# A two-layer SiLU block on one core: matmuls that reuse the weights already loaded

## The chip, the core and the metric

The kernel runs on one core of a Trainium2 chip. TensorE multiplies a stationary operand ("weights", loaded by an instruction of its own) with a moving operand and writes into PSUM, which has 8 banks of 512 fp32 columns here. ScalarE (ACT) and VectorE (DVE) read PSUM and write SBUF. The SP and ACT queues issue DMAs. The metric is the device time of one execution in microseconds; the time before is the median of three runs.

## The reference

The inputs are bf16: x is 1 x 2048 x 640 (S = 2048 tokens, D = 640), w1 is 640 x 1728, w2 is 1728 x 640 (F = 1728).

```python
def reference(x, w1, w2):
    h = jnp.einsum("bsd,df->bsf", x, w1)
    h = _silu(h)
    out = jnp.einsum("bsf,fd->bsd", h, w2)
    return out
```

## The kernel before

All operands stay in SBUF. `xT` holds x transposed, 5 blocks of 128 rows of D by 2048 tokens. `w1s` holds w1 in 5 such blocks. h is kept transposed: `hT` has 13 tiles of 128 rows of F by 2048 tokens, and the last 64 rows of F go to `hTt`, two chunks side by side in the two halves of the partitions. w2 is `w2s` (13 tiles of 128 rows) and `w2t` (the last 64 rows, loaded twice, once in each half).

**First product.** The tokens are taken in four chunks of 512 (`SCH`). Chunk 0 is interwoven with the loads of w1. Then one loop runs over chunks 1, 2 and 3: for each of 13 tiles of F it takes a bank, issues 5 matmuls (one for each block of D; the w1 tile is the stationary operand, 512 columns of `xT` the moving one), and a Silu on ACT writes the tile of `hT`. `wait(pe, ld_xc[c])` ahead of each chunk waits for that chunk's five x transposes, which SP issues early on, chunk after chunk (line 158). The last 64 rows of F follow for all chunks (`h_tail`), two chunks at a time in the two halves of the array's columns.

**Second product, last 128 columns (`Wide`).** For each chunk, `Wide(c)` computes the last 128 of 640 output columns, transposed: the stationary operand is a half tile of w2 (64 rows by 128 columns), the moving one 512 tokens of `hT`. Two units run at once, one on rows 0 to 63 of the array (r0 = 0) and one on rows 64 to 127 (r0 = `HP`), each into its own bank. Each unit must see both halves of every tile, so it makes two passes: `begin` with one half and then its 64-row `tail`, whose last matmul ticks `halfway`; `rest` with the other half. The second pass of a unit must not start before its first has been written, which is what `wait(pe, X.halfway, Y.halfway)` in `quad` is for. `quad` runs the first pass of units 0 and 1, the first pass of 2 and 3, then the second pass of 0 and 1, and the second pass of 2 and 3, closing each unit behind its second pass. `close` copies the bank to `oT` (`evac` alternates between DVE and ACT), and SP transposes it by DMA into `o_sb` (line 275).

**Second product, first 512 columns (`Tok`).** For each block of 128 tokens the stationary operand is a tile of `hT` and the moving one 512 columns of w2. Three quads of half-row units follow, and the last four blocks use whole rows, the very last split in 384 and 128 columns. Each block is copied and stored; a store waits for its chunk's output transpose (`st_w`).

The order of the work is written out by hand: each engine takes its instructions in program order, and every dependence is a semaphore wait by `wait`. `bank()` hands out the 8 banks in turn and makes PE wait until the last reader of the bank is done. All matmuls are recorded under line 170, in `mm`. Each `pe.matmul` becomes two instructions, a weight load and a matmul.

Of the kernel before, what the change touches and what calls it, by code (L numbers as in the profile page):

```python
# [9 lines left out]
def bass_standalone__dense_activation_silu__prompt_kernel(  # L10
# [11 lines left out]
    S, D = xf.shape  # L22
    F = w1.shape[1]
    P = 128
    NB = 8
    BANK = 512
    DT = D // P
    FT = F // P
    FL = F - FT * P
    SCH = 512  # L30
    HB = 256
    NSC = S // SCH
    DA = 512
# [4 lines left out]
    pe, act, dve, pool, sp = nc.tensor, nc.scalar, nc.vector, nc.gpsimd, nc.sync  # L38

    with ExitStack() as es:  # L40
        def sb(name, shape, dtype):
            return es.enter_context(nc.sbuf_tensor(name, shape, dtype))

        xT = sb("xT", [P, DT, S], bf16)
        w1s = sb("w1s", [P, DT, F], bf16)
        w2s = sb("w2s", [P, FT, D], bf16)
        w2t = sb("w2t", [P, D], bf16)
        hT = sb("hT", [P, FT, S], bf16)
        hTt = sb("hTt", [P, NSC // 2, SCH], bf16)
# [4 lines left out]
        ps = es.enter_context(nc.psum_tensor("ps", [P, NB, BANK], fp32))  # L54
# [4 lines left out]
        def sem(name):  # L59
            s = es.enter_context(nc.semaphore(name))  # L60
            count[s.name if hasattr(s, "name") else name] = 0
            return [s, 0]

        def tick(ins, s, n=1):
            ins.then_inc(s[0], n)
            s[1] += n
            return (s, s[1])

        def wait(eng, *points):
            for pt in points:  # L70
                if pt is None:
                    continue
                s, v = pt
                key = (id(eng), id(s))
                if seen.get(key, 0) < v:
                    eng.wait_ge(s[0], v)
                    seen[key] = v

        s_pe, s_act, s_dve = sem("s_pe"), sem("s_act"), sem("s_dve")
# [74 lines left out]
        ld_xc = {}  # L154
# [14 lines left out]
        def mm(o, l, r, start, stop, shared=False):  # L169
            return pe.matmul(o, lhsT=l, rhs=r, start=start, stop=stop, skip_group_check=shared)  # L170

        def silu(out_ap, in_ap, bank, after):
            wait(act, after)
            r = tick(act.activation(out=out_ap, in_=in_ap, func=ACT.Silu), s_act)  # L174
            bank_free[bank] = r
            return r

        def part(k, ft, c0, c1, start=False, stop=False):
            return mm(ps[:, ft, c0:c1], w1s[:, k, ft * P:(ft + 1) * P], xT[:, k, c0:c1],
                      start, stop, shared=True)  # L180
# [14 lines left out]
        for ft in range(NO):  # L195
            t = tick(part(4, ft, 0, SCH, stop=True), s_pe)
            silu(hT[:, ft, 0:SCH], ps[:, ft, :], ft, t)
# [3 lines left out]
        def bank():  # L201
            b = nxt[0] % NB
            nxt[0] += 1
            wait(pe, bank_free[b])
            return b

        wait(pe, ld_rest)
        for ft in range(NO, FT):
            b = bank()
            if ft == NO + 2:  # L210
                wait(pe, ld_rest2)
            for k in range(DT):
                ins = mm(ps[:, b, :], w1s[:, k, ft * P:(ft + 1) * P], xT[:, k, 0:SCH],
                         start=(k == 0), stop=(k == DT - 1))
            silu(hT[:, ft, 0:SCH], ps[:, b, :], b, tick(ins, s_pe))
        for c in range(1, NSC):
            wait(pe, ld_xc[c])
            for ft in range(FT):
                b = bank()
                for k in range(DT):  # L220
                    ins = mm(ps[:, b, :], w1s[:, k, ft * P:(ft + 1) * P],
                             xT[:, k, c * SCH:(c + 1) * SCH], start=(k == 0), stop=(k == DT - 1))
                h_last = silu(hT[:, ft, c * SCH:(c + 1) * SCH], ps[:, b, :], b, tick(ins, s_pe))
        h_tail = []
        for q in range(NSC // 2):
            b = bank()
            for k in range(DT):
                for hh in range(2):
                    c = 2 * q + hh
                    ins = mm(ps[hh * FL:(hh + 1) * FL, b, :], w1s[:, k, F0:F],  # L230
                             xT[:, k, c * SCH:(c + 1) * SCH],
                             start=(k == 0), stop=(k == DT - 1), shared=True)
# [16 lines left out]
        HP = P // 2  # L249
# [4 lines left out]
        class Wide:  # L254
# [3 lines left out]
            def open(self):  # L258
                self.b = bank()

            def half(self, r0, ft, start, stop):
                c = self.c
                return mm(ps[:, self.b, :], w2s[r0:r0 + HP, ft, DA:D],
                          hT[r0:r0 + HP, ft, c * SCH:(c + 1) * SCH], start, stop, shared=True)

            def tail(self):
                q, r0 = self.c // 2, (self.c % 2) * FL
                return mm(ps[:, self.b, :], w2t[r0:r0 + FL, DA:D], hTt[r0:r0 + FL, q, :],
                          False, False, shared=True)

            def close(self, t):
                c = self.c
# [44 lines left out]
        def lanes(up, down):  # L317
            for i in range(max(len(up), len(down))):
                for lane in (up, down):
                    if i < len(lane):  # L320
                        lane[i]()

        def begin(u, r0):
            def end():
                wait(pe, *h_tail)
                u.halfway = tick(u.tail(), s_pe)
            return [lambda ft=ft: u.half(r0, ft, ft == 0, False) for ft in range(FT)] + [end]

        def rest(u, r0, done):
            ops = [lambda ft=ft: u.half(r0, ft, False, ft == FT - 1) for ft in range(FT - 1)]  # L330
            ops.append(lambda: done.append(tick(u.half(r0, FT - 1, False, True), s_pe)))
            return ops

        def quad(A, B, C, E):
            A.open()
            B.open()
            lanes(begin(A, 0), begin(B, HP))
            C.open()
            E.open()
            lanes(begin(C, 0), begin(E, HP))  # L340
            for X, Y in ((A, B), (C, E)):
                dx, dy = [], []
                wait(pe, X.halfway, Y.halfway)
                lanes(rest(Y, 0, dy), rest(X, HP, dx))
                X.close(dx[0])
                Y.close(dy[0])

        wait(pe, *ld_w2)
        wait(pe, h_last)
        quad(Wide(0), Wide(1), Wide(2), Wide(3))  # L350
        last = None
        for q in range(NSC // 2):
            for j in range(0, JB, 2):
# [12 lines left out]
        for u, eng in ((A, dve), (B, act), (C, act), (E, dve), (G2, act)):  # L366
            for ft in range(FT):
                ins = u.whole(ft, ft == FT - 1)
# [31 lines left out]
```

## Time and profile before

| | |
|---|---|
| median of three runs | 124.97 us (124.93 to 125.05) |
| profiled execution | 124.80 us |
| its span, first to last instruction | 123.2 us |
| TensorE busy | 120.9 us, 797 matmuls and 797 weight loads |
| chunks 2 and 3 of the first product | 32.1 to 60.1 us |
| last-column units | 62.7 to 74.4 us |

The profile is one execution of the program. PE is the matmul row, PEld the weight loads, SPq and ACTq the DMA queues. Each group of instructions has its line, engine, operation, output and inputs, its count, busy time and mean duration, and the idle time of the engine just before with what ended it. The recorded end of a matmul is modelled, and consecutive matmuls overlap in the record (each lasts some 0.38 us, and they start closer together than that), so their distance from start to start is what counts. A slot here means the time from one matmul start to the next, where matmuls that run at the same time in two halves of the array are one slot.

### The profile page before, as it was taken

Reading aid. Unit: us, or ns where it says so; the run is one execution under the profiler, and the core shown is the slowest. Engines: PE = TensorE matmul, PEld = TensorE weight load, DVE = VectorE, ACT = ScalarE, POOL = GpSimd, SP = SyncE. Lnnn points to the kernel's source line nnn. Section 1 sums busy time; section 2 is a strip of 40 time slices with the busy share of each in tenths; the row PEclk is TensorE's granted clock in tenths of the full one; section 3 lists DMA queues with packets and bytes.
Section 4 is the critical chain, followed back from the end, with each engine's and each line's share of the span. In section 5 each row is a group of like instructions: output and inputs, shape, how many; then the busy total and the mean of one; then the engine's idle time right before and its main releaser. Section 6 shows DMA issues by size and latency. Waiting matters only on the chain.

```text
span 123.2 us, 1779 instructions
## 1 busy us (share of the span) xinstructions
PE 120.9 (98%) x797; PEld 55.5 (45%) x797; DVE 6.8 (6%) x11; ACT 38.8 (31%) x67; POOL 0.3 (0%) x5
## 2 busy tenths in 40 slices
PE   8999999999999999999999999999999999999993
PEld 6344444444444444444444444444444444444452
DVE  0000000000000000000000022002201300222001
ACT  4002975555555555555530011001101200110110
POOL 1000000000000000000000000000000000000000
PEclk9999999999999999999999999999999999999999
DMA  6999845445990000000000004202200220022122
GB/s 141 238 255 306 162 112 94 97 93 101 345 366 10 0 5 0 3 0 0 0 0 5 0 13 113 50 0 106 106 0 5 106 106 0 5 106 106 53 74 86
DMA packets 19479, 10.38 MB, mean 84 GB/s; under 512 B 13456, under 2 KB 18960, under 8 KB 19472
## 3 DMA queue, kind: packets, MB, share of 16 engines
q1 hardware_dynamic: 19184, 10.05, 31.1%
q10 hardware_dynamic: 288, 0.23, 0.7%
q8 instruction: 6, 0.10, 0.3%
q14 instruction: 1, 0.01, 0.0%
HBM read 4.51 MB, written 2.62 MB: 58 GB/s over the span
## 4 chain that ended last, share of the span: by engine, by line
PE 94%; DMA 3%; ACT 0%; issue 0%
PE ps L170 94%; DMA w1s<-in_w_dram 3%; ACT o_sb L244 0%
## 5 line engine op out<-in xcount | busy, mean ns | idle before, releaser
L170 PE MATMUL ps<-xT,w1s 128*128 128x512 bf16 (+1 forms) x280 | 59.1, 381 | 0.1
L170 PE MATMUL ps<-w2s,hT 64*128 64x512 bf16 (+3 forms) x377 | 46.2, 369 | 0.0
L170 PEld LDWEIGHTS ps<-xT,w1s 128*128 128x128 bf16 (+1 forms) x280 | 26.4, 99 | 32.7 <-DMA w1s<-in_w_dram 0.8
L174 ACT ACTIVATE hT<-ps 128x512 bf16<-128x512 f32 x52 | 30.0, 608 | 28.9 <-PE ps L170 28.9
L170 PEld LDWEIGHTS ps<-w2s,hT 64*128 64x128 bf16 (+1 forms) x377 | 21.0, 95 | 24.2 <-issue 0.2
L244 ACT CAST o_sb<-ps 128x512 bf16<-128x512 f32 (+1 forms) x9 | 4.9, 550 | 41.5 <-PE ps L170 41.5
L170 PE MATMUL ps<-hT,w2s 64*128 64x512 bf16 x104 | 11.7, 376 | 0.0
L170 PEld LDWEIGHTS ps<-hT,w2s 64*128 64x128 bf16 x104 | 5.0, 94 | 6.3 <-issue 0.4
L242 DVE CAST o_sb<-ps 128x512 bf16<-128x512 f32 (+1 forms) x8 | 5.4, 675 | 40.5 <-PE ps L170 40.5
L242 DVE CAST oT<-ps 128x512 bf16<-128x512 f32 x2 | 1.4, 692 | 73.7 <-PE ps L170 73.7
L244 ACT CAST oT<-ps 128x512 bf16<-128x512 f32 x2 | 1.2, 585 | 10.6 <-PE ps L170 10.6
L130 PE MATMUL ps<-z 128*128 128x256 bf16 x15 | 3.4, 419 | 0.4 <-DVE z L124 0.4
L170 PE MATMUL ps<-w2t,hTt 64*128 64x512 bf16 (+2 forms) x17 | 2.9, 363 | 0.0
L130 PEld LDWEIGHTS ps<-z 128*128 128x128 bf16 x15 | 2.1, 147 | 1.2 <-DVE z L124 0.4
L174 ACT ACTIVATE hTt<-ps 128x512 bf16<-128x512 f32 x2 | 1.2, 597 | 1.1 <-PE ps L170 1.1
L152 ACT ACT_TABLE_LOAD x1 | 1.3, 1283 | 0.7 <-PEq L385 0.7
L170 PEld LDWEIGHTS ps<-w2t,hTt 64*128 64x128 bf16 x17 | 0.9, 94 | 1.1
L170 PE MATMUL ps<-hTt,w2t 64*128 64x512 bf16 x4 | 0.8, 376 | 0.0
L170 PEld LDWEIGHTS ps<-hTt,w2t 64*128 64x128 bf16 x4 | 0.2, 94 | 0.2
L152 ACT ACTIVATE warm<-warm 128x32 f32<-128x32 f32 x1 | 0.2, 229 | 0.0
L139 POOL MEMSET warm<- 128x32 f32 x1 | 0.1, 124 | 0.3 <-POOLq L385 0.3
L385 POOL MEMSET const-bfloat16-1.0<- 128x1 bf16 x1 | 0.1, 101 | 0.0
(4 smaller groups left out, 0.4 us busy)
## 6 DMA issues: line engine op xcount, KB each, us to landing
out_dram<-o_sb SPq DMA_DIRECT2D x15, 160.0 KB, 1.8
w2s<-in_w_dram SPq DMA_DIRECT2D x1, 1120.0 KB, 6.4
w1s<-in_w_dram SPq DMA_DIRECT2D x4, 256.0 KB, 3.9
w2s<-in_w_dram SPq DMA_DIRECT2D x1, 960.0 KB, 8.6
w1s<-in_w_dram SPq DMA_DIRECT2D x1, 560.0 KB, 6.4
w1s<-in_w_dram SPq DMA_DIRECT2D x1, 320.0 KB, 5.2
xT<-in_x_dram SPq DMA_TRANSPOSE x18, 3.7
w1s<-in_w_dram ACTq DMA_DIRECT2D x1, 160.0 KB, 2.5
```

What stands on the lines that cost most here:

```text
L130: pe.matmul(ps[:, 3, 0:HB], lhsT=z[:, 0:1].broadcast_to([P, P]), rhs=z[:, 0:1].broadcast_to([P, HB]), start=True, stop=True)
L139: p_warm = tick(pool.memset(warm[:, :], 0.0), s_pool)
L152: act.activation(out=warm[:, :], in_=warm[:, :], func=ACT.Silu)
L170: return pe.matmul(o, lhsT=l, rhs=r, start=start, stop=stop, skip_group_check=shared)
L174: r = tick(act.activation(out=out_ap, in_=in_ap, func=ACT.Silu), s_act)
L242: r = tick(dve.tensor_copy(out=out_ap, in_=in_ap), s_dve)
L244: r = tick(act.copy(out=out_ap, in_=in_ap), s_act)
L385: nc = _bacc.Bacc("TRN2", target_bir_lowering=False, num_devices=1)
```

## The change

A new helper `held` emits a matmul without a weight load, so that it uses the weights that the matmul before it (on the same rows) left in the array. It is used in two places. In the first product, chunk 1 keeps its loop, and chunks 2 and 3 are taken together: for each tile of F two banks, and for each block of D one matmul with its load for chunk 2 and one `held` for chunk 3. PE waits for the x of both chunks ahead of the first tile, and the two Silu of a tile follow its last matmul.

The last-column units no longer go through `quad`. `wides` runs all four at once: for each tile, units 0 and 1 with loads on the two row halves, then units 2 and 3 `held` on the same halves; then the four tails in the same manner; then one wait for `halfway` of all four; then the second pass with the halves exchanged, and the four `close` at the end. The other quads are as before.

```diff
+        def held(o, l, r, start, stop, shared=False):
+            rows = l.shape[0]
+            r0 = l.base_partition()
+            return pe.add_instruction(mybir.InstMatmult(
+                name=nc.get_next_instruction_name(),
+                ins=[pe.lower_ap(r), pe.lower_ap(l)],
+                outs=[pe.lower_ap(o)],
+                start_tensor_calc=start, stop_tensor_calc=stop,
+                tile_size=(rows, P), tile_position=(r0, 0), ldweights=False,
+                bass_skip_group_check=shared,
+            ))
...
-        for c in range(1, NSC):
-            wait(pe, ld_xc[c])
-            for ft in range(FT):
-                b = bank()
-                for k in range(DT):
-                    ins = mm(ps[:, b, :], w1s[:, k, ft * P:(ft + 1) * P],
+        wait(pe, ld_xc[1])
...
+        wait(pe, ld_xc[2], ld_xc[3])
+        for ft in range(FT):
+            pair = [(c, bank()) for c in (2, 3)]
+            done = []
+            for k in range(DT):
+                for op, (c, b) in zip((mm, held), pair):
+                    ins = op(ps[:, b, :], w1s[:, k, ft * P:(ft + 1) * P],
                              xT[:, k, c * SCH:(c + 1) * SCH], start=(k == 0), stop=(k == DT - 1))
-                h_last = silu(hT[:, ft, c * SCH:(c + 1) * SCH], ps[:, b, :], b, tick(ins, s_pe))
+                    if k == DT - 1:
+                        done.append(tick(ins, s_pe))
+            for (c, b), t in zip(pair, done):
+                h_last = silu(hT[:, ft, c * SCH:(c + 1) * SCH], ps[:, b, :], b, t)
...
+        def wides():
+            us = [Wide(c) for c in range(NSC)]
+            for u in us:
+                u.open()
+            for ft in range(FT):
+                for u, r0, hold in ((us[0], 0, 0), (us[1], HP, 0), (us[2], 0, 1), (us[3], HP, 1)):
+                    u.half(r0, ft, ft == 0, False, hold)
+            wait(pe, *h_tail)
+            for u, r0, hold in ((us[0], 0, 0), (us[1], HP, 0), (us[2], 0, 1), (us[3], HP, 1)):
+                u.halfway = tick(u.tail(hold), s_pe)
+            wait(pe, *[u.halfway for u in us])
+            done = []
+            for ft in range(FT):
+                for u, r0, hold in ((us[1], 0, 0), (us[0], HP, 0), (us[3], 0, 1), (us[2], HP, 1)):
+                    t = u.half(r0, ft, False, ft == FT - 1, hold)
+                    if ft == FT - 1:
+                        done.append((u, tick(t, s_pe)))
+            for u, t in done:
+                u.close(t)
+
         wait(pe, *ld_w2)
         wait(pe, h_last)
-        quad(Wide(0), Wide(1), Wide(2), Wide(3))
+        wides()
```

`Wide.half` and `Wide.tail` take an argument `hold` that picks `held` instead of `mm`.

More of the change, by code (lines that the diff above doesn't have):

```diff
@@ L215, in bass_standalone__dense_activation_silu__prompt_kernel @@
             silu(hT[:, ft, 0:SCH], ps[:, b, :], b, tick(ins, s_pe))
-        for c in range(1, NSC):
-            wait(pe, ld_xc[c])
-            for ft in range(FT):
-                b = bank()
-                for k in range(DT):
-                    ins = mm(ps[:, b, :], w1s[:, k, ft * P:(ft + 1) * P],
+        wait(pe, ld_xc[1])
+        for ft in range(FT):
+            b = bank()
+            for k in range(DT):
+                ins = mm(ps[:, b, :], w1s[:, k, ft * P:(ft + 1) * P],
+                         xT[:, k, SCH:2 * SCH], start=(k == 0), stop=(k == DT - 1))
+            silu(hT[:, ft, SCH:2 * SCH], ps[:, b, :], b, tick(ins, s_pe))
+        wait(pe, ld_xc[2], ld_xc[3])
+        for ft in range(FT):
+            pair = [(c, bank()) for c in (2, 3)]
+            done = []
+            for k in range(DT):
+                for op, (c, b) in zip((mm, held), pair):
+                    ins = op(ps[:, b, :], w1s[:, k, ft * P:(ft + 1) * P],
                              xT[:, k, c * SCH:(c + 1) * SCH], start=(k == 0), stop=(k == DT - 1))
-                h_last = silu(hT[:, ft, c * SCH:(c + 1) * SCH], ps[:, b, :], b, tick(ins, s_pe))
+                    if k == DT - 1:
+                        done.append(tick(ins, s_pe))
+            for (c, b), t in zip(pair, done):
+                h_last = silu(hT[:, ft, c * SCH:(c + 1) * SCH], ps[:, b, :], b, t)
         h_tail = []
@@ L259, in open, with half, tail @@
                 self.b = bank()
-            def half(self, r0, ft, start, stop):
+            def half(self, r0, ft, start, stop, hold=False):
                 c = self.c
-                return mm(ps[:, self.b, :], w2s[r0:r0 + HP, ft, DA:D],
-                          hT[r0:r0 + HP, ft, c * SCH:(c + 1) * SCH], start, stop, shared=True)
-            def tail(self):
+                return (held if hold else mm)(
+                    ps[:, self.b, :], w2s[r0:r0 + HP, ft, DA:D],
+                    hT[r0:r0 + HP, ft, c * SCH:(c + 1) * SCH], start, stop, shared=True)
+            def tail(self, hold=False):
                 q, r0 = self.c // 2, (self.c % 2) * FL
-                return mm(ps[:, self.b, :], w2t[r0:r0 + FL, DA:D], hTt[r0:r0 + FL, q, :],
-                          False, False, shared=True)
+                return (held if hold else mm)(
+                    ps[:, self.b, :], w2t[r0:r0 + FL, DA:D], hTt[r0:r0 + FL, q, :],
+                    False, False, shared=True)
             def close(self, t):
@@ L346, in quad @@
                 Y.close(dy[0])
+        def wides():
[10 more added lines that the diff above has]
+            done = []
+            for ft in range(FT):
+                for u, r0, hold in ((us[1], 0, 0), (us[0], HP, 0), (us[3], 0, 1), (us[2], HP, 1)):
[4 more added lines that the diff above has]
+                u.close(t)
         wait(pe, *ld_w2)
         wait(pe, h_last)
-        quad(Wide(0), Wide(1), Wide(2), Wide(3))
+        wides()
         last = None
```

## The prediction

> **What bounds the kernel now.** I read the page's busy table and slices first, then the chain that ended last, then the stages one by one.
>
> ```profile
> PE 120.9 (98%) x797; PEld 55.5 (45%) x797; DVE 6.8 (6%) x11; ACT 38.8 (31%) x67; POOL 0.3 (0%) x5
> PE   8999999999999999999999999999999999999993
> PEclk9999999999999999999999999999999999999999
> PE 94%; DMA 3%; ACT 0%; issue 0%
> L170 PE MATMUL ps<-xT,w1s 128*128 128x512 bf16 (+1 forms) x280 | 59.1, 381 | 0.1
> L170 PEld LDWEIGHTS ps<-xT,w1s 128*128 128x128 bf16 (+1 forms) x280 | 26.4, 99 | 32.7 <-DMA w1s<-in_w_dram 0.8
> ```
>
> TensorE is busy nearly everywhere, and its matmuls are 94% of the chain. The weight loads (PEld) last 99 ns each but have a row of their own beside the matmuls; whether they cost anything is seen only in the distance from one matmul to the next. So I asked for the stages: first chunks 1, 2 and 3 of the first product, then the last-column units.
>
> ```profile
> 18.05:32.08 14.03, 14.03 (x66) 6.37 (x65) 0.00 (x0) 7.76 (x13) 0.00 (x0) 1.00 0.56 118
> 32.08:46.11 14.03, 14.03 (x67) 6.37 (x65) 0.00 (x0) 7.76 (x13) 0.00 (x0) 1.00 0.36 132
> 46.11:60.13 14.02, 14.02 (x66) 6.37 (x65) 0.00 (x0) 7.76 (x13) 0.00 (x0) 1.00 0.00 1
> 62.72:74.40 11.68, 11.68 (x112) 5.28 (x111) 0.69 (x1) 1.18 (x2) 0.00 (x0) 1.00 0.05 13
> ```
>
> Columns: the stretch, its length, then PE, weight loads, DVE, ACT and POOL busy, the granted clock, DMA share and rate. Each chunk is 65 matmuls in 14.03 us, 215.8 ns apart, with TensorE never idle, at full clock.
>
> ```profile
> 62.41 0.38 PE L170 MATMUL ps<-xT,w1s 128*64 128x512 bf16 x2
> 62.73 2.98 PE L170 MATMUL ps<-hT,w2s 64*128 64x512 bf16 x26
> ...
> 68.57 0.38 PE L170 MATMUL ps<-hTt,w2t 64*128 64x512 bf16 x2
> 68.78 5.78 PE L170 MATMUL ps<-hT,w2s 64*128 64x512 bf16 x52
> ```
>
> This is the timeline of PE alone over the last-column units. Half tiles run two at a time, one in each half of the rows (the starts in the trace lie 3 ns apart), so 52 matmuls are 26 slots: (5.78 - 0.38)/25 = 0.216 us, the same spacing. The `halfway` waits between the passes leave no gap (68.57 to 68.78), because a whole pass of the other pair stands between the tail that ticks and the half that waits for it. The one gap is at 62.41 to 62.73: 0.31 us where 0.216 would do, at the change from column halves to row halves.
>
> **What a weight load costs now.** Single matmul starts in the last tile stand 55.8 ns apart with 128 columns, 162.5 with 384; the chunks have 215.8 with 512. The slope is (215.8 - 55.8)/384 = 0.417 ns per column, so 512 columns are 213.3 ns and 2.5 ns remain whatever the width. That remainder is all that a hidden weight load could be costing: a load starts about 2 ns after the matmul before it, needs 94 to 98 ns, and is ready over 100 ns ahead. What the change can win is bounded by it.
>
> **The change, part by part.**
>
> 1. *Loads removed.* 13 tiles x 5 = 65 in the first product and, of the 54 slots of the last-column units, 27 (54 loads). That makes 92 load-free slots. Upper end of the gain: 92 x 2.5 = 0.23 us. Lower end: nothing, if the 2.5 ns belong to the matmul. A loss is not excluded, since no row shows a matmul without a load; its nearest rows are 11 ns (the second slot after a break comes 227 ns after the first, in the starts at 62.73 and 62.96) and 96 ns (the break at 62.41 itself). I take nothing: the cold dummies at the start, 256 columns, stand 213.3 ns apart, exactly 256 columns at twice that slope, though each has a load of 152 ns. So a load with its exchange does not by itself add time to a slot; the 2.5 ns look like a hand-over from matmul to matmul.
>
> The Trainium skill ("TensorE: Matmul & The Clock Gate", section "Wait — 56ns, not 53.3ns?") speaks against the change: it calls about 2.5 ns a fixed cost per matmul, downstream of decode. By it the loads are worth 0 of the 0.23 us; were the 2.5 ns the load's, the sum below would be 0.23 us lower. The spacing agrees with its size, and no row of before shows whose it is.
>
> 2. *Chunks 2 and 3 together.* The wait for chunk 3's x moves up to 32.1 us, from 46.1. Its last transpose is issued at 27.3 us and the trace's semaphore events show it landed at 30.4: 1.7 us to spare, cost nothing. It costs the same 1.7 us of cover if x comes late. No DMA moves. A pair takes 2.16 us on PE and needs two Silu of 0.6 us: ACT keeps up. A bank comes round after four pairs, three pairs (6.5 us) after its matmuls end, and its Silu is done within 0.42 + 1.2 us: no wait. The last Silu of chunk 3 follows that of chunk 2 and ends near 61.5 instead of 61.15 us; the next reader starts at 62.73, behind the 2 us of tail matmuls. Nothing.
>
> 3. *The four last-column units in one interleave.* The number of slots stays 54. But the tails of all four units now stand right before the second pass, which waits for `halfway` of all four: TensorE waits for its own last matmul to be written. This drain is new. Its price: in the trace the semaphore event of a 64-row matmul comes 390 ns after its start. A weight load that waits starts 43 ns after the event (the loads released by w1: event 5.259, load 5.301), and the matmul 4 ns later. So the next slot comes 437 ns after the tail instead of 216, and the slot after it 10 ns late as above: +0.23 us. That is the lower end, with all waits on one load. But the four waits are on four values: before, a second wait on PE stands as a semaphore instruction of its own ahead of the load (51 ns each, released 28 ns after its event), and one such instruction holds back the sequencer, so the queue behind it is empty when it is let go. With one or two of them behind the event: 390 + 28 + 51 + a dispatch of up to 105 ns (event instruction at 13.631, next load at 13.736) + 4 - 216 + 10 = 0.27 to 0.37 us. I take 0.28, nearest to the first. Queued behind the waiting load are the second pass and all Tok units, and nothing covers it, as TensorE is the chain from 5.3 to 121.3 us. A lower bound from another kind of break, the 0.096 + 0.011 us of the change of tiling at 62.41, would be 0.11 us.
>
> The Trainium skill ("TensorE: Matmul & The Clock Gate", section "The cost: per-tile semaphore tail") has increments of several tiles write one after another, about 26 ns each. With four increments, of which two come with the last slot, an estimate by it is up to 0.05 us more. The events here, 390 and 387 ns after the starts of a pair 3 ns apart, show no such step.
>
> 4. *Evacuation of the four units.* All four end together near 74.5 us: two copies each on DVE (0.69) and ACT (0.585), done by 76.3 us. Their banks are opened again at 85.8 us. On SP the four output transposes (1.24 us to issue, 2.4 to land) start near 75.5 instead of 72.5 and land by 83 us at the latest; the first store queued behind them goes at 84.2. Nothing, with 1 us or more of cover; what waits for a late one is a store, not TensorE.
>
> **The sum.** 0 (loads) + 0 + 0.28 (drain) + 0 = +0.28 us. The profiled execution took 124.80 us (span 123.2, 1.6 around it), so 125.08 for it; the median before is 0.17 higher, 124.97, and 125.25 is the forecast: 0.22% slower. A measurement of this kernel can tell about 0.2%, that is 124.72 to 125.22.
>
> **The rivals.**
>
> - *The 2.5 ns go with the load.* For it: it is a constant per slot, as a swap of weights would be. Against: the cold dummies. 124.97 + 0.28 - 0.23 = 125.02, not slower. From 0.3 ns per load-free slot on, the forecast falls inside 0.2%; it can never reach faster with the drain in place.
> - *The drain is cheap.* If the four waits end like the change of tiling (0.11 us), 125.08, or 124.85 with the whole gain. For it: TensorE knows its own drain there. Against: the wait is a semaphore, and ACT's copies start 0.41 us after the matmuls that they wait for. No drain at all and the whole gain would be 124.74.
> - *A matmul without a load costs more*, because the next load is not fetched ahead over it, or the two row halves no longer run together. For it: no row shows the form. Against: a load needs only 98 of 216 ns. With 11 ns per slot 92 x 11 = 1.0 us, 126.25; with 96 ns 8.8 us, 134.
> - *x of chunk 3 is late*: 1.7 us of cover must be gone first; 2% at most.
>
> **Chances and range.** Forecast (drain, no gain) 0.47, of which 0.12 lies inside 0.2%, since 0.25 us is within the bounds of the drain, 0.23 to 0.37; gain with the load 0.27, inside; cheap drain 0.10, inside but for 0.03 faster; dearer matmul 0.14 and x late 0.02, slower. Slower 0.35 + 0.16 = 0.51, inside 0.12 + 0.27 + 0.07 = 0.46, faster 0.03. The range reaches from 124.85 (cheap drain with the gain) to 125.9 (half of the 11 ns per slot on top of 0.37).
>
> **What would show it.** Weight loads fall from 797 to 678. The window of chunks 2 and 3 shows 28.05 us if I am right, 27.89 if the 2.5 ns go. The last-column units show one idle time of the weight loads, of about 0.2 to 0.3 us, near 68.5 us, released by PE, and the stage is 11.95 us instead of 11.67. The output transposes start about 3 us later. I am wrong if the spacing of load-free matmuls is not 216 ns, if there is no gap near 68.5, or if a wait of TensorE stands at 32.1 us or in the pairs.

## The result and the profile after

The changed kernel takes 125.59 us (median of 14 runs, 125.14 to 126.12) against 124.97 us before: a ratio of 1.0047, 95% interval 1.003 to 1.0065, so 0.37 to 0.81 us slower. Its profiled execution took 125.22 us, 0.42 us more than the profiled one of before.

The busy rows of the page after:

```profile
PE 120.7 (98%) x791; PEld 49.4 (40%) x678; DVE 6.7 (5%) x11; ACT 37.3 (30%) x67; POOL 0.3 (0%) x5
L170 PEld LDWEIGHTS ps<-xT,w1s 128*128 128x128 bf16 (+1 forms) x215 | 20.2, 99 | 38.9 <-issue 22.8
L175 PE MATMUL ps<-xT,w1s 128*128 128x512 bf16 x65 | 24.6, 379 | 0.2
L170 PE MATMUL ps<-hT,w2s 64*128 64x512 bf16 x52 | 10.1, 377 | 0.3 <-PE ps L175 0.3
```

119 weight loads are gone, as the change says (797 to 678; of the matmuls 6 records are missing). A new line stands there: a matmul of the last-column units waited 0.3 us for PE itself. The stages of after, chunks 2 and 3 first and then the last-column units (columns as before: stretch, length, then PE, weight loads, DVE, ACT and POOL busy, clock, DMA; the second stretch ends before the stage does):

```profile
32.08:60.13 28.05, 27.89 (x129) 6.36 (x65) 0.00 (x0) 13.62 (x25) 0.00 (x0) 1.00 0.20 71
62.71:74.63 11.92, 11.66 (x110) 2.86 (x56) 0.00 (x0) 0.60 (x1) 0.00 (x0) 1.00 0.00 1
```

Chunks 2 and 3 run through the same window as before. PE shows 27.89 busy of 28.05 us there, but the hole is that of missing records (three of the matmuls have none, and their neighbours stand 432 ns apart, twice the spacing); that it is the figure which the prediction named for a saving is chance. From the first matmul start of the two chunks to the last it is 27.84 us (129 distances) in both traces. Half of the matmuls have no load now, and they are 215.8 ns apart all the same. The last-column units have a real hole, 0.26 us; from their first matmul to the first of the token blocks the trace has 12.08 us, where before has 11.67 and the prediction had 11.95. Here is PE's timeline of after around it, and below the same place on the row of the weight loads:

```profile
68.34 0.38 PE L170 MATMUL ps<-hTt,w2t 64*128 64x512 bf16 x2
68.56 0.38 PE L175 MATMUL ps<-hTt,w2t 64*128 64x512 bf16 x2
69.19 0.39 PE L170 MATMUL ps<-hT,w2s 64*128 64x512 bf16 x2 [0.26 <-PE ps L175]
69.41 0.39 PE L175 MATMUL ps<-hT,w2s 64*128 64x512 bf16 x2
```

```profile
69.16 0.36 PEld L170 LDWEIGHTS ps<-hT,w2s 64*128 64x128 bf16 x4 [0.94 <-PE ps L175]
```

From the second slot of tails to the first slot of the second pass 635 ns go by (68.557 to 69.192 in the trace), where a slot is 216. That is 0.42 us more than a slot. From the first last-column matmul to the last matmul of the kernel the trace has 58.371 us before and 58.803 us after: +0.432 us. Ahead of that stage and behind the last matmul the two profiled executions agree to 0.02 us.

The trace's semaphore events (the times at which a semaphore's count rises) and instructions show what the 635 ns are made of. The four tails start at 68.341, 68.343, 68.557 and 68.559; their events come at 68.731, 68.765, 68.947 and 68.977. The four values that `wait` names stand in three waiting instructions ahead of the second pass. A semaphore instruction goes through at 68.975 (28 ns after the third event), another with two values at 69.086, the waiting load at 69.162, the load for the other half of the rows at 69.194, and the first matmul at 69.192. So the 635 ns are 390 (tail to third event) + 28 + 111 + 76 + 30. The events are all there at 68.977, and the first matmul starts 0.215 us later; with a single wait (an experiment below) it starts 0.046 us after the last event.

### The profile page after: what moved, and what is told of

Same layout as the page of the kernel before. It is cut to its first block, busy times and chain, and to the rows that moved or that the text cites. A ratio compares the mean times of both kernels' runs of the same rounds, so it can differ in the third digit from the quotient of the medians.

```text
span 123.7 us, 1666 instructions
## 1 busy us (share of the span) xinstructions
PE 120.7 (98%) x791; PEld 49.4 (40%) x678; DVE 6.7 (5%) x11; ACT 37.3 (30%) x67; POOL 0.3 (0%) x5
## 3 DMA queue, kind: packets, MB, share of 16 engines
q1 hardware_dynamic: 19184, 10.05, 32.1%
## 4 chain that ended last, share of the span: by engine, by line
PE 98%; issue 1%; ACT 0%; DVE 0%
PE ps L170 78%; PE ps L175 16%; PE ps L130 3%; ACT o_sb L267 0%; DVE z L124 0%
## 5 line engine op out<-in xcount | busy, mean ns | idle before, releaser
L170 PE MATMUL ps<-xT,w1s 128*128 128x512 bf16 (+1 forms) x210 | 54.4, 383 | 0.1
L186 ACT ACTIVATE hT<-ps 128x512 bf16<-128x512 f32 x52 | 28.6, 605 | 30.6 <-PE ps L170 30.6
L170 PEld LDWEIGHTS ps<-xT,w1s 128*128 128x128 bf16 (+1 forms) x215 | 20.2, 99 | 38.9 <-issue 22.8
L170 PEld LDWEIGHTS ps<-w2s,hT 64*128 64x128 bf16 (+1 forms) x377 | 23.3, 95 | 22.0 <-issue 0.5
L175 PE MATMUL ps<-xT,w1s 128*128 128x512 bf16 x65 | 24.6, 379 | 0.2
L170 PE MATMUL ps<-hT,w2s 64*128 64x512 bf16 x52 | 10.1, 377 | 0.3 <-PE ps L175 0.3
L175 PE MATMUL ps<-hT,w2s 64*128 64x512 bf16 x52 | 10.0, 376 | 0.0
L170 PEld LDWEIGHTS ps<-hT,w2s 64*128 64x128 bf16 x52 | 2.7, 94 | 8.8 <-issue 7.6
```

The source lines that it names most:

```text
L175: return pe.add_instruction(mybir.InstMatmult(name=nc.get_next_instruction_name(), ins=[pe.lower_ap(r), pe.lower_ap(l)], outs=[pe.lower_ap ...
```

## The experiments

The theory after the result, called D: the drain ahead of the second pass is the whole loss, and a load-free slot costs what a slot with a load costs. The rival L: the load-free matmuls themselves cost or save something, since the median moved by 0.62 us and the drain explains 0.43.

### Chunks 2 and 3 alone

```diff
-        wides()
+        quad(Wide(0), Wide(1), Wide(2), Wide(3))
```

> Chunks 2 and 3 share w1 loads as in the changed kernel, the last-column units go through quad as before (65 loads fewer, no new wait). Theory D (the whole loss is the drain of TensorE before the second pass of the last-column units, 0.42 us in the changed kernel's trace; a load-free slot costs what a loaded one does): 215.8 ns from matmul to matmul in chunks 2 and 3, no gap near 68.5 us, 124.97 us, level with before. Rival L (a load-free matmul itself costs or saves): a saving of 2.5 ns a slot would give 124.8; if the 0.2 us of the loss that the drain does not account for lie in the pairs, 125.1 to 125.2.

Measured: 125.09 us against 124.96 on the same chip, ratio 1.0014 (0.9995 to 1.0033). The window of the two chunks:

```profile
32.40:60.45 28.05, 28.05 (x132) 6.34 (x65) 0.00 (x0) 13.62 (x25) 0.00 (x0) 1.00 0.18 64
```

65 loads instead of 130, and 28.05 us as before with no hole. PE goes from the tails into the second pass without a gap:

```profile
68.88 0.38 PE L170 MATMUL ps<-hTt,w2t 64*128 64x512 bf16 x2
69.09 0.59 PE L170 MATMUL ps<-hT,w2s 64*128 64x512 bf16 x4
```

From the first last-column matmul to the last matmul it is 58.370 us. So this half of the change is worth nothing either way. The interval of the ratio contains 1, and no stage that the edit touches shows the median's 0.13 us.

### The last-column units with all their loads

```diff
-                for u, r0, hold in ((us[0], 0, 0), (us[1], HP, 0), (us[2], 0, 1), (us[3], HP, 1)):
+                for u, r0, hold in ((us[0], 0, 0), (us[1], HP, 0), (us[2], 0, 0), (us[3], HP, 0)):
...
-            for u, r0, hold in ((us[0], 0, 0), (us[1], HP, 0), (us[2], 0, 1), (us[3], HP, 1)):
+            for u, r0, hold in ((us[0], 0, 0), (us[1], HP, 0), (us[2], 0, 0), (us[3], HP, 0)):
...
-                for u, r0, hold in ((us[1], 0, 0), (us[0], HP, 0), (us[3], 0, 1), (us[2], HP, 1)):
+                for u, r0, hold in ((us[1], 0, 0), (us[0], HP, 0), (us[3], 0, 0), (us[2], HP, 0)):
```

> As the changed kernel, but all four last-column units load their half tile themselves: 54 loads more, the order of the units and the one wait ahead of the second pass stay. Theory D: the same gap of 0.635 us from slot to slot ahead of the second pass, and the changed kernel's time, 125.4 to 125.6 us. Rival L: if the load-free half-row matmuls cause the loss, the gap shrinks to 0.22 us and the time goes to 125.0.

Measured: 125.44 us against 124.96, ratio 1.0044 (1.0024 to 1.0063). PE's timeline of it:

```profile
68.80 0.59 PE L170 MATMUL ps<-hTt,w2t 64*128 64x512 bf16 x4
69.68 0.59 PE L170 MATMUL ps<-hT,w2s 64*128 64x512 bf16 x3 [0.29 <-PE ps L170]
```

The 54 loads are back and the gap is too, 665 ns (30 more than in the changed kernel: the second semaphore instruction comes 141 ns after the first instead of 111). The stage to the last matmul is 58.833 us, 0.46 more than before. The loss does not need the load-free matmuls of these units.

### The kernel before with the wait alone

```diff
-        def quad(A, B, C, E):
+        def quad(A, B, C, E, drain=False):
...
+                if drain:
+                    wait(pe, A.halfway, B.halfway, C.halfway, E.halfway)
                 wait(pe, X.halfway, Y.halfway)
...
-        quad(Wide(0), Wide(1), Wide(2), Wide(3))
+        quad(Wide(0), Wide(1), Wide(2), Wide(3), True)
```

`wait` adds nothing for a value that is no higher than one the engine has waited for, so the new line acts once, ahead of the first pair's second pass.

> The kernel before, with all its loads and its order, but ahead of the second pass of the first pair of last-column units TensorE waits for the tails of all four. Theory D: this wait alone makes the loss, a gap of 0.55 to 0.64 us near 68.6 us and 125.35 to 125.6 us. Rival L: the loss needs the load-free matmuls; gap or not, clearly under the changed kernel.

Measured: 125.59 us against 125.08 on its chip, ratio 1.0040 (1.0021 to 1.0060). Its timeline on PE:

```profile
68.88 0.38 PE L170 MATMUL ps<-hTt,w2t 64*128 64x512 bf16 x2
69.52 0.61 PE L170 MATMUL ps<-hT,w2s 64*128 64x512 bf16 x4 [0.26 <-PE ps L170]
```

The gap is 636 ns and the stage 58.803 us, which is that of the changed kernel to the nanosecond. The kernel before, with all its 797 loads and its own order, becomes as slow as the changed one by this wait alone.

### One wait instead of four

```diff
-            wait(pe, *[u.halfway for u in us])
+            wait(pe, us[3].halfway)
```

> As the changed kernel, with the four tails still ticking, but TensorE waits for the last of the four values alone (the others are lower values of the same semaphore). Theory D, read from the changed kernel's semaphore events: the last event comes 420 ns after the start of the tail slot, a load that waits starts 43 ns later, its matmul 4 ns after that: gap 0.467 instead of 0.635 us, so 0.17 us less than the changed kernel. Rival S (the sequencer's refill after the drain is what costs, however many waits there are): the gap stays above 0.58 us.

The gap, on PE:

```profile
69.38 0.38 PE L175 MATMUL ps<-hTt,w2t 64*128 64x512 bf16 x2
69.85 0.39 PE L170 MATMUL ps<-hT,w2s 64*128 64x512 bf16 x2
```

It is 465 ns as expected (467) and well under rival S's 0.58 us, and the stage 58.633 us, 0.17 less than in the changed kernel. The time was a miss: 125.71 us against 124.96 (6 runs, ratio 1.0059, 1.0036 to 1.0083), where 0.17 us less than the changed kernel was expected; of these 0.75 us the stage holds 0.26. The profiled execution (125.87 us) shows that run's excess ahead of the stage: the last-column units begin at 63.54 us instead of 62.73. The weight loads of the start show where it arises, here in this run and then in before:

```profile
5.53 0.15 PEld L170 LDWEIGHTS ps<-xT,w1s 128*128 128x128 bf16 x1 [0.28 <-DMA w1s<-in_w_dram]
5.96 0.15 PEld L170 LDWEIGHTS ps<-xT,w1s 128*128 128x128 bf16 x1 [0.28 <-issue]
6.35 1.61 PEld L170 LDWEIGHTS ps<-xT,w1s 128*128 128x128 bf16 x8 [0.24 <-issue]
```

```profile
4.06 0.15 PEld L170 LDWEIGHTS ps<-xT,w1s 128*128 128x128 bf16 x1 [0.27 <-issue]
4.44 0.31 PEld L170 LDWEIGHTS ps<-xT,w1s 128*128 128x128 bf16 x2 [0.23 <-issue]
```

A load lasts 0.15 us, with matmuls of 512 columns up to 427 ns apart, until 6.3 us in the one and until 4.4 in the other; later loads last 0.10 us and matmuls are 216 ns apart. So the first product ran at half its pace until 1.9 us later in this execution, before it reached anything that the edit touches. The five other runs of it have times but no trace, so whether the same holds for its median is not shown, and the miss in time stays open.

### One tick and one wait

```diff
-                u.halfway = tick(u.tail(hold), s_pe)
-            wait(pe, *[u.halfway for u in us])
+                t = u.tail(hold)
+            wait(pe, tick(t, s_pe))
```

> As the changed kernel, but only the last of the four tails ticks and TensorE waits for that one value. Theory D: without the increments written one after another (30 ns between the last two in the changed kernel) the event comes at 390 ns, the gap is 0.437 us, 0.03 less than with four ticks and one wait and 0.20 less than the changed kernel. Rival S: above 0.58 us as there.

```profile
68.69 0.38 PE L175 MATMUL ps<-hTt,w2t 64*128 64x512 bf16 x2
69.13 0.39 PE L170 MATMUL ps<-hT,w2s 64*128 64x512 bf16 x2
```

The gap is 440 ns (437 expected): the one event comes 392 ns after its matmul's start, the load 41 ns after the event, the matmul 5 later. The stage is 58.606 us, 0.235 more than before. The time, 125.11 us against 124.96, ratio 1.0016 (0.9997 to 1.0035), is too coarse to tell so small a loss; the trace tells it. This is the cheapest drain of these runs. The other 0.20 us of the changed kernel's 0.43 were the price of writing and waiting for four values where one says it all. So rival S, by which the gap stays above 0.58 us however many waits there are, falls.

### The drain covered

Between the tails and the second pass, the first pass of the first two token units (14 slots) runs; all four values are still waited for, and the first token quad later goes on from there.

```diff
             for u, r0, hold in ((us[0], 0, 0), (us[1], HP, 0), (us[2], 0, 1), (us[3], HP, 1)):
                 u.halfway = tick(u.tail(hold), s_pe)
+            X, Y = Tok(0), Tok(JB)
+            X.open()
+            Y.open()
+            lanes(begin(X, 0), begin(Y, HP))
             wait(pe, *[u.halfway for u in us])
```

> As the changed kernel, but the first pass of the first two token units (27 slots) is put between the tails of the last-column units and their second pass; all four values are still waited for. Theory D: the drain is covered, no gap ahead of the second pass (216 ns), and with load-free slots worth nothing the time is that of before, 124.97 us (within 0.1). Rival L (load-free slots cost something): the gap goes too, but the time stays 0.2 us above before.

The 27 slots named there are a miscount: the trace has 28 matmuls in 14 slots, two at a time.

Measured: 124.85 us against 125.08, ratio 0.9985 (0.9967 to 1.0004). The timeline on PE:

```profile
68.81 0.38 PE L170 MATMUL ps<-hTt,w2t 64*128 64x512 bf16 x2
69.02 0.38 PE L175 MATMUL ps<-hTt,w2t 64*128 64x512 bf16 x2
69.24 0.81 PE L170 MATMUL ps<-w2s,hT 64*128 64x512 bf16 x6
```

No gap, and 58.370 us from the first last-column matmul to the last matmul: level with before to a nanosecond, with 119 loads fewer. The 0.23 us by which its median lies under before's is not a gain that a stage of its trace shows, and its interval contains 1.

### Many more matmuls without loads

The kernel before, where in chunks 1 to 3 only the first of a tile's five matmuls loads weights, and in the last four token blocks only the first of a unit's 13. The right weights of the others are left out; the work in columns is the same.

```diff
-                    ins = mm(ps[:, b, :], w1s[:, k, ft * P:(ft + 1) * P],
+                    ins = (held if k else mm)(ps[:, b, :], w1s[:, k, ft * P:(ft + 1) * P],
...
-                return mm(ps[:, self.b, 0:self.e - self.a], hT[:, ft, st * P:(st + 1) * P],
+                return (held if ft else mm)(ps[:, self.b, 0:self.e - self.a], hT[:, ft, st * P:(st + 1) * P],
```

> The kernel before, where in chunks 1 to 3 only the first of the five matmuls of a tile loads weights, and in the last four token blocks only the first of the 13 of a unit: the right weights of the others are left out, 156 + 60 loads fewer and as many load-free slots, 2.3 times those of the changed kernel, 12 of them only 128 columns wide. Theory D with a per-matmul remainder: 215.8 ns at 512 columns and 55.8 at 128, loaded or not, 124.97 us. Rival L2 (the 2.5 ns are the load's): 213.3 and 53.3 ns, 0.54 us less, 124.4. Rival L (a load-free matmul costs): more than 125.3.

Measured: 124.95 us against 125.08, ratio 0.9985 (0.9964 to 1.0006). The page's busy row, and PE at the last tile:

```profile
PE 120.8 (98%) x791; PEld 35.1 (28%) x581; DVE 6.8 (6%) x11; ACT 38.8 (31%) x67; POOL 0.3 (0%) x5
```

```profile
120.69 0.22 PE L170 MATMUL ps<-w2s,hT 128*128 128x128 bf16 x1
120.75 0.83 PE L175 MATMUL ps<-w2s,hT 128*128 128x128 bf16 x12
```

Twelve matmuls of 128 columns without a load: (0.83 - 0.22)/11 = 55 ns, and by the single starts 0.670 us over twelve distances, 55.8 ns, exactly as in before, where each has a load. From the first matmul of chunks 1 to 3 to the last, 194 distances, both before and this one have 41.872 us, and the stage from the last-column units on is 58.371 us in both. The loads are worth nothing even at 128 columns, the narrowest matmuls tried here.

The stage that the change touches, side by side (from the first last-column matmul to the last matmul, start to start, in the trace):

| version | gap ahead of the second pass, ns | stage, us | median and before on its chip, us |
|---|---|---|---|
| before | 216 | 58.371 | 124.97 |
| changed kernel | 635 | 58.803 | 125.59 / 124.97 |
| chunks 2 and 3 alone | 216 | 58.370 | 125.09 / 124.96 |
| units with loads | 665 | 58.833 | 125.44 / 124.96 |
| before with the wait | 636 | 58.803 | 125.59 / 125.08 |
| one wait | 465 | 58.633 | 125.71 / 124.96 |
| one tick, one wait | 440 | 58.606 | 125.11 / 124.96 |
| drain covered | 216 | 58.370 | 124.85 / 125.08 |
| many load-free | 216 | 58.371 | 124.95 / 125.08 |

## Why the prediction was right, and where its size was off

The forecast was 125.25 us with 124.85 to 125.9; 125.59 was measured. The direction and its mechanism are shown by the wait alone in the kernel before; one term was too small. By that term's own bounds (0.23 to 0.37 us) the time would have been 125.20 to 125.34 us. The stated range holds 125.59 only because it also made room for half of a dearer matmul, which did not come; that part was luck.

- *Loads removed: 0 of at most 0.23 us.* Right, but not by the reason given. The dummies, 213.3 ns apart at twice the slope, show no remainder of 2.5 ns at all, so they could not tell whose it is at full pace. The runs do: the 2.5 ns that remain per slot belong to the matmul, since they stand unchanged with 216 load-free matmuls, at 128, 384 and 512 columns (55.8, 162.5 and 215.8 ns). Here the rule of the Trainium skill ("TensorE: Matmul & The Clock Gate", section "Wait — 56ns, not 53.3ns?"), a fixed cost per matmul, and the runs agree. The first rival (the 2.5 ns go with the load) and the third (a matmul without a load costs more) are both out: the slot is 215.8 ns with and without.
- *Chunks 2 and 3 together: nothing.* Right. No wait of TensorE stands at 32.1 us; the last x of chunk 3 landed at 30.5 us by the semaphore events. The fourth rival, x of chunk 3 late, is out with it.
- *The drain: 0.28 us, with bounds of 0.23 and 0.37.* This is the step that failed, in size: it measured 0.43 us, outside both bounds. The lower end stood for all four waits on one load; it is met (0.235) only with one tick as well, and four ticks with one wait take 0.262, because the last event then comes 417 ns after its matmul instead of 392. What the sum had too small was the rest. I had 51 ns for a semaphore instruction, a dispatch of up to 105 and 4 from the load to its matmul, 160 ns at most; in the trace the first such instruction is let go at 68.975 and the second only 111 ns later, though all four events are there by 68.977, the load 76 ns after that, and its matmul 30 ns behind it, 217 ns. That fits a queue that is empty and is filled one instruction at a time (the loads of the two halves start 32 ns apart, and 2 with one wait), but this reading was not tested by itself. One wait instead of four gives 0.17 us back, one tick instead of four another 0.025.
- *The increments.* I weighed the rule of the Trainium skill ("TensorE: Matmul & The Clock Gate", section "The cost: per-tile semaphore tail") that increments are written one after another, about 26 ns each, against a pair of events that I took for simultaneous, and left it out. The events of the tails come 34 and 30 ns apart, so they do follow one another here, at a little more than the page's figure. My row was misread: I had taken the next event after each start, which was the same event for both matmuls of a pair; the trace of before has them 34 ns apart too (65.936 and 65.970 us).
- *Evacuation: nothing.* Right: the output transposes start at 75.5 us as forecast, the last lands at 81.8 us, and the first store behind them is issued at 84.6.
- *The cheap drain* (0.11 us, as at the change of tiling) is out: no version in which the wait stands uncovered is under 0.235.

The profiled executions differ by 0.42 us, the medians by 0.62 with an interval from 0.37. The drain of 0.43 lies inside; whether the other 0.19 are more than the scatter of the start is not settled, but no stage of the trace holds them, and the same wait in the kernel before measured 0.51.

## What to carry to other kernels

Before a weight load is taken out, look at the distance from one matmul start to the next at several widths: what is left of it beside the time of the columns is all that a load can be costing. Here that was 2.5 ns a slot, and leaving loads out won none of it. Ask instead what the new order puts side by side: a pass that waited for something done long ago may now wait for the instruction just before it, and on an engine that is never idle that latency, less the slot that it replaces, is new time. Where such a wait must stay, put other work between, or at least tick once and wait once: the last value of a semaphore contains the earlier ones. Named in rising order, as here, four values made three waiting instructions; named alone, the last made one. No run leaves the wait out, so whether the sums need it is not shown here.

## What the runs showed that I had not expected

- Three waiting instructions in a row on PE took 0.17 us more than one wait for the last value (635 and 465 ns). So a wait for a value that a later one contains is not free when TensorE has run out of work; in the kernel before, where such waits come while matmuls are still under way (a semaphore instruction at 66.433 us), they leave no gap.
- The scatter from run to run (before: 124.46 to 125.67 us on one chip) does not lie in the later stages of the executions that were traced. The time from the last-column units on is the same to 1 ns in the four traces without a gap (58.370 and 58.371 us), while the nine profiled executions begin it between 62.72 and 63.54 us. In eight of them the matmuls of the first product go from up to 427 to 216 ns apart at a moment between 4.4 and 6.3 us from the start of the span. In the ninth, with one tick and one wait, the last slow load is at 2.9 us, ahead of the first product, and yet its units begin at 62.85 us, after holes ahead of 4.0 and 5.4 us; so the pace is not the whole of it. A difference of 0.1 or 0.2 us in the medians here is read better in the stages.
